# A transformer block on one core: states of batches 4 to 7 made two groups ahead, behind the output products of the next batch

## The chip, the core and the metric

The kernel runs on one NeuronCore of a Trainium2 chip. The metric is the device time of one execution in microseconds (us), the median of the runs. In names, PE is TensorE (matmul), PEld its weight loads, DVE is VectorE, ACT is ScalarE, POOL is GpSimd and SP is SyncE, whose queue issues nearly all the transfers here. [...]

## The reference

Linear attention without softmax, a norm per head, and then a gated feed-forward layer. Cut to what matters:

```python
def _attn_ref(q, k, v, g_norm):                    # (8 batches, 8 heads, 576 rows, 64)
    kv = np.einsum('bhsd,bhse->bhde', k, v)        # the state: 64 x 64 per batch and head
    out = np.einsum('bhsd,bhde->bhse', q, kv)      # the output products
    rms = np.sqrt(np.mean(out * out, axis=-1, keepdims=True) + 1e-06)
    return out / rms * g_norm

def _moe_ref(x, w_gate, w_val, w_out, rms_g):      # x: (4608, 512)
    rms = np.sqrt(np.mean(x * x, axis=-1, keepdims=True) + 1e-06)
    xn = x / rms * rms_g
    g = xn @ w_gate                                # 512 -> 1536
    silu = g * (1.0 / (1.0 + np.exp(-g)))
    val = xn @ w_val                               # 512 -> 1536
    return silu * val @ w_out                      # 1536 -> 512
```

The 4608 rows are the 8 batches of 576 rows, with the 8 heads of 64 side by side.

## The kernel before

**Groups.** The feed-forward layer works on groups of 512 rows. Group n, for n from 0 to 7, is the first 512 rows of batch n; group 8 is the 64 last rows of all eight batches together. Group 0 and the start-up have their own code; the change and the steps of the prediction lie in the end of group 0 and in groups 1 to 8, which run in the loop at L990.

**Units.** A group has 12 units of up products (`Ffn.up`, L471) and 4 of down products (`Ffn.down`, L554). Unit j makes 128 of the 1536 columns: four matmuls into a gate bank `g_ps`, four into a value bank `v_ps` (L477), each 128x128 weights on 512 columns. ACT makes `silu` from the gate bank (L482), and DVE multiplies it with the value bank into `h_sb` (L483). The gate and the value banks rotate in twos (`gps_pool`, `vps_pool`), so unit j+2 can't write its gate bank before ACT has read that of unit j, nor its value bank before DVE has read that of unit j. Each of the 4 down units is 12 matmuls into a bank `o_ps` (L529), copied by ACT to `o_sb` (L104, called from L537).

**Attention of the next group, in between.** While group n runs, the attention of batch n+1 is made in pieces, in steps that stand behind the units. `steps[u]` lists what is emitted after unit u. The order is written out by hand (a manual schedule), and each engine takes its instructions in the order in which they are emitted.

- `kv_products` (L277): the state, 72 small matmuls of 64x64 tiles (L286) from `kb` and `vb` into two banks. `kv_copy` (L291) then copies it to `kv_all`, half by ACT and half by DVE, in two copies of 64 rows each (L295).
- `o_products` (L305): 32 small matmuls with 64 rows of weights (L326), from `qt` (q turned) and `kv_all`, into two `att_ps` and two `o_ps` banks.
- `put_squares` and `put_rows` (L336, L343): ACT reads those banks twice, for squares and for the rows. `sums` (L351): DVE makes a product and a sum from the squares (L355, L356). `head`, `guess`, `root` and `scale` (L358 to L375) are the norm on DVE, and `x_rows` (L377) turns the result by transfers into `xnt`, the input of group n+1.

Before the change, in groups 2 to 6 the state of batch n+1 is made behind unit 1 and its output products behind unit 2. In group 1 it is units 2 and 4. Group 8's attention, the `tail`, has no state of its own, since it uses those of all batches.

**Inputs.** In step 2 of group n, `load_batch` loads q, k and v of batch n+2 in fp32 into three of seven stage buffers. In steps 11 to 15 of the same group ACT casts them to bf16: q in step 11, k in 12 and 13, v in 14 and 15. The bf16 k and v have two buffers each, for even and for odd batches.

Of the kernel before, what the change touches and what calls it, by code (L numbers as in the profile page):

```python
# [10 lines left out]
FP32 = mybir.dt.float32  # L11
# [9 lines left out]
def kernel(  # L21
# [14 lines left out]
    B, H, S, D = q.shape  # L36
# [8 lines left out]
    NS = d_model // 128  # L45
# [5 lines left out]
    def pool(name, bufs, **kw):  # L51
        return ctx.enter_context(tc.tile_pool(name=name, bufs=bufs, **kw))
# [16 lines left out]
    gps_pool = pool("gps", 2, space=PS)  # L69
    vps_pool = pool("vps", 2, space=PS)  # L70
    ops_pool = pool("ops", 2, space=PS)
    att_pool = pool("att", 2, space=PS)
# [3 lines left out]
    PE, DVE, SC, GP = nc.tensor, nc.vector, nc.scalar, nc.gpsimd  # L76
# [22 lines left out]
    def stage(n=2048):  # L99
        return stage_pool.tile([128, NS * C * D], FP32, name="st")[:, 0:n]  # L100

    def cast(engine, dst, src):
        if engine is SC:
            engine.copy(out=dst, in_=src)  # L104
        else:
            engine.tensor_copy(out=dst, in_=src)  # L106
# [7 lines left out]
    def alloc_kv(b, name):  # L114
        raws[b, name] = stage(NS * C * D).rearrange("p (j x) -> p j x", j=NS)

    def load_kv(b, name, queue, js=slice(0, NS)):
        view = srcs[name][b].rearrange("h s d -> (h s d)").rearrange("(j p x) -> p j x", j=NS, p=128)
        queue.dma_start(out=raws[b, name][:, js, :], in_=view[:, js, :])

    def cast_kv(b, name, j, engine):

        cast(engine, bufs[b][name][:, j].rearrange("p c d -> p (c d)"), raws[b, name][:, j, :])
# [7 lines left out]
    def load_q(b):  # L131
        st = stage()
        raws[b, "q"] = st
        for hs in (slice(0, 4), slice(4, 8)) if b == 1 else (slice(0, H),):
            nc.sync.dma_start(
                out=st.rearrange("p (h x) -> p h x", h=H)[:, hs],
                in_=q[b, hs, 0:MAIN, :].rearrange("h (p t) d -> p h (t d)", t=T),
            )

    def alloc_q(b):  # L140
        bufs[b]["q"] = qb_pool.tile([128, T, H, D], BF16, name="qb")
# [10 lines left out]
    def cast_q(b, i, engine):  # L152

        cast_heads(b, i, 2, 4, engine)

    def load_batch(b):
        load_q(b)
        for name in ("k", "v"):
            alloc_kv(b, name)
            load_kv(b, name, nc.sync)  # L160
# [34 lines left out]
    def load_wo(blk, parts=(0, 2)):  # L195
        if ("o", blk) not in w_st:
            w_st["o", blk] = stage().rearrange("p (c d) -> p c d", d=d_model)
        for i in parts:
            nc.sync.dma_start(
                out=w_st["o", blk][:, i : i + 2, :], in_=wo_view[:, 4 * blk + i : 4 * blk + i + 2, :]  # L200
            )
# [66 lines left out]
    class Att:  # L268
# [5 lines left out]
            self.sq = {}  # L274
            self.qt = None

        def kv_products(self):  # L277

            self.kv_ps = [att_pool.tile([128, 2, D], FP32, name="att_ps") for _ in range(2)]
            kb, vb = bufs[self.n]["k"], bufs[self.n]["v"]  # L280
            for a in range(2):
                for c in range(C):
                    for x in range(2):
                        for g in range(2):
                            rows, to = slice(g * D, g * D + D), slice((g ^ x) * D, (g ^ x) * D + D)
                            PE.matmul(  # L286
                                self.kv_ps[x][to, a, :], lhsT=kb[rows, 2 * a + x, c, :], rhs=vb[rows, 2 * a + x, c, :],
                                start=(a == 0 and c == 0), stop=(a == 1 and c == C - 1),
                            )
# [372 lines left out]
    def state0(j, dummies):  # L662
        ps = att_pool.tile([128, 512], FP32, name="att_ps")
        warm(ps, max(dummies, 1), 512 if dummies else 128)
        kv_pair(ps[:, 0:128], j)
        return ps
# [38 lines left out]
    kv0 = state0(0, 0)  # L705
# [96 lines left out]
    load_q(1)  # L802
    load_wo(1)
    load_wo(2)
    load_batch(2)

    def broadcast_gsq():
        ps = att_pool.tile([128, 512], FP32, name="att_ps")
# [86 lines left out]
    def f_x(c, x, engine):  # L895
        bank = att_pool.tile([128, NS, 128], BF16, name="att_ps")
        to_rows(x, 1, c, bank, engine)

    pools = ("ops", "ops", "g", "v")

    def down_part(c, lo, hi):
        ffn.down_products(c, lo, hi, pools[c])
# [44 lines left out]
    atts = {b: Att(b) for b in range(2, B + 1)}  # L947
    for c in range(T):
        atts[2].q_rows(c)
    down_part(1, 8, 12)  # L950
    f_x(0, xs[0], SC)
    f_x(1, xs[1], SC)
# [9 lines left out]
    def load_q_tails():  # L962
        st = stage().rearrange("p (c x) -> p c x", c=T)
        for b in range(B):
            u = b % 2
            nc.sync.dma_start(
                out=st[u * TAIL : (u + 1) * TAIL, b // 2].rearrange("r (h d) -> r h d", h=H),
                in_=q[b, :, MAIN:S, :].rearrange("h r d -> r h d"),
            )
        tails_q["raw"] = st  # L970
        tails_q["b"] = qb_pool.tile([128, T, H, D], BF16, name="qb").rearrange("p t h d -> p t (h d)")

    def cast_q_tails(i, engine):
        dst, src = (tails_q[nm].rearrange("p c (h d) -> p c h d", h=H) for nm in ("b", "raw"))
        cast(engine, dst[:, :, place(i) : H : 4, :], src[:, :, i:H:4, :])
# [7 lines left out]
    def turn_q_tails(c):  # L983
        if c == 0:
            tails_q["t"] = qt_pool.tile([128, NS, MAIN], BF16, name="qt").rearrange("p j (c t) -> p c j t", c=T)
        nc.sync.dma_start_transpose(out=tails_q["t"][:, c], in_=tails_q["b"][:, c, :])
# [3 lines left out]
    for n in range(1, B + 1):  # L990
        ffn = Ffn(n)
        steps = {u: [] for u in range(NF + T)}
        if n + 2 < B:
            steps[2].append(lambda n=n: load_batch(n + 2))
        if n == B - 3:
            load_q_tails()
        if n == 1:
            steps[0] += [lambda i=i: cast_kv(2, "k", i, DVE) for i in (2, 3)]
            steps[0] += [lambda i=i: cast_kv(2, "v", i, GP) for i in (0, 1)]
            steps[1] += [lambda i=i: cast_kv(2, "v", i, DVE) for i in (2, 3)]  # L1000
        if n == 3:
            steps[3] += [cross_states]
        if n < B:
            a = atts[n + 1]
            kv0, o0 = (2, 4) if n == 1 else (1, 2)
            if not a.tail:
                steps[kv0] += [a.kv_products, a.kv_copy]
            steps[o0] += [a.o_products]
            for i in range(2):
                u = o0 + 2 * i  # L1010
                steps[u] += [lambda a=a, i=i: a.put_squares(i)]
                steps[u + 1] += [lambda a=a, i=i: a.put_rows(i)]
                for c in range(2):
                    steps[u + i + c] += [lambda a=a, c=2 * i + c: a.sums(c)]
            late = 2 * int(n == 1)
            steps[8 + late] += [a.head]
            steps[9 + late] += [a.guess, a.root]
            for c in range(T):
                steps[10 if c == 0 and not late else 11] += [lambda a=a, c=c: a.scale(c), lambda a=a, c=c: a.x_rows(c)]
        b = n + 2  # L1020
        if b < B:
            steps[10] += [lambda b=b: alloc_q(b)]
            for i in range(T):
                steps[11] += [lambda b=b, i=i: cast_q(b, i, SC)]
            for i in range(NS):
                steps[12 + i // 2] += [lambda b=b, i=i: cast_kv(b, "k", i, SC)]
                steps[14 + i // 2] += [lambda b=b, i=i: cast_kv(b, "v", i, SC)]
            for c in range(T):
                steps[13].append(lambda b=b, c=c: atts[b].q_rows(c))
        if b == B:  # L1030
            for i in range(T):
                steps[11] += [lambda i=i: cast_q_tails(i, SC)]
            for c in range(T):
                steps[13].append(lambda c=c: turn_q_tails(c))
        for unit in range(NF + T):
            if unit < NF:
                ffn.up(unit)
            elif n == B and unit == NF + T - 1:
                ffn.down_last(unit - NF)
            else:  # L1040
                ffn.down(unit - NF)
            for step in steps[unit]:
                step()
# [30 lines left out]
```

## Time and profile before

| what | value |
|---|---|
| time, median of 3 runs | 319.03 us (318.98 to 319.62) |
| span of the profiled execution | 317.6 us |
| granted TensorE clock, mean | 0.998 |
| start of groups 2, 3, 4, 5, 6, 7, 8 | 87.82, 120.39, 152.97, 185.54, 218.11, 250.68, 282.53 us |
| up and down matmuls (L477, L529), ns of one in the records | 379 |
| start to start of such matmuls in a row | 216 ns |
| one silu on ACT (L482) | 597 ns |
| one product on DVE (L483) | 684 ns |
| one sum on DVE (L356) | 1220 ns |
| one copy of half a state's half, ACT / DVE | 260 / 288 ns |
| one cast of k or v on ACT, 128x576 | 673 ns |

How to read it: a matmul's record lasts 379 ns because records of matmuls overlap; what a matmul costs in a row is the 216 ns from one start to the next. A group of 144 such matmuls needs 31.1 us, and groups 2 to 6 start 32.57 us apart, so that about 1.5 us of a group is something else.

### The profile page before, as it was taken

The numbers are of one execution on the slowest core, as the hardware profiler recorded it, in microseconds if no ns is written. First come the engines' busy times: TensorE is split into PE (matmuls) and PEld (weight loads), VectorE is DVE, ScalarE is ACT, GpSimd is POOL, SyncE is SP. The second block draws the span as 40 slices with busy tenths as digits, with TensorE's granted clock in tenths as the row PEclk, the third lists the DMA queues.
The fourth block names the chain that finished last, engine by engine and source line by source line (L and its number), as shares of the span: only waits on it lengthen the run. The fifth ranks groups of instructions, "written<-read, shape, count | busy, mean of one in ns | idle before, by whom it ended". The sixth has DMA issues, their size and how long they took to land.

```text
span 317.6 us, 5996 instructions
## 1 busy us (share of the span) xinstructions
PE 308.5 (97%) x2334; PEld 150.3 (47%) x2371; DVE 181.3 (57%) x378; ACT 175.6 (55%) x323; POOL 21.5 (7%) x46
## 2 busy tenths in 40 slices
PE   7899999999999999999999999999999999999995
PEld 3575446444444444444444444444444444444443
DVE  3776768679339922893289327941795079504310
ACT  3577367485667465746683768376745374233321
POOL 1174351100000000000000000000000000000000
PEclk9999999999999999999999999999999999999999
DMA  7999999685369267904790489939002710230014
GB/s 266 358 385 388 375 375 333 145 275 215 90 180 344 86 138 187 369 9 108 189 378 22 98 172 207 354 66 181 22 0 60 140 66 3 57 141 3 0 33 100
DMA packets 60712, 54.95 MB, mean 173 GB/s; under 512 B 36232, under 2 KB 45708, under 8 KB 60684
## 3 DMA queue, kind: packets, MB, share of 16 engines
q1 hardware_dynamic: 60304, 53.92, 56.7%
q10 hardware_dynamic: 380, 0.66, 0.6%
q8 instruction: 18, 0.29, 0.4%
q14 instruction: 10, 0.08, 0.1%
HBM read 37.75 MB, written 9.44 MB: 149 GB/s over the span
## 4 chain that ended last, share of the span: by engine, by line
PE 90%; DMA 5%; SPq 1%; another core or an unknown queue 1%; issue 1%; POOL 1%; DVE 0%; ACT 0%
PE v_ps L477 28%; PE g_ps L477 28%; PE o_ps L529 26%; DMA st<-in_moe_w_val_dram 3%; DMA st<-in_q_dram 2%; PE att_ps L286 2%; PE v_ps L529 1%; PE g_ps L529 1%; DMA out_dram<-o_sb 1%; PE att_ps L326 1%; PE o_ps L494 1%; POOL wv_sb L191 1%; PE o_ps L326 0%; PE att_ps L262 0%
## 5 line engine op out<-in xcount | busy, mean ns | idle before, releaser
L483 DVE TENSOR_TENSOR h_sb<-silu,v_ps 128x512 bf16<-128x512 bf16 x104 | 71.1, 684 | 99.9 <-ACT silu L482 68.1
L477 PE MATMUL v_ps<-xnt,wv_sb 128*128 128x512 bf16 x409 | 106.2, 379 | 0.7
L477 PE MATMUL g_ps<-xnt,wg_sb 128*128 128x512 bf16 x398 | 104.6, 379 | 0.7
L482 ACT ACTIVATE silu<-g_ps 128x512 bf16<-128x512 f32 x104 | 62.1, 597 | 70.1 <-PE g_ps L477 58.4
L529 PE MATMUL o_ps<-wo_sb,h_sb 128*128 128x512 bf16 x386 | 86.8, 379 | 0.4
L477 PEld LDWEIGHTS <-wv_sb 128*128 128x128 bf16 x416 | 40.7, 98 | 49.1
L529 PEld LDWEIGHTS <-h_sb 128*128 128x128 bf16 x420 | 40.6, 98 | 47.6 <-issue 0.4
L477 PEld LDWEIGHTS <-wg_sb 128*128 128x128 bf16 x416 | 39.5, 98 | 46.4
L104 ACT COPY o_sb<-o_ps 128x512 f32<-128x512 f32 (+1 forms) x34 | 19.6, 581 | 40.2 <-PE o_ps L529 36.6
L373 DVE TENSOR_TENSOR xna<-outa,s1y 128x512 bf16<-128x512 bf16 x28 | 17.9, 685 | 0.0
L104 ACT CAST qb<-st 128x512 bf16<-128x512 f32 (+1 forms) x30 | 16.2, 603 | 3.0 <-DMA st<-in_q_dram 3.0
L104 ACT CAST vb<-st 128x576 bf16<-128x576 f32 x25 | 15.7, 673 | 3.4 <-DMA st<-in_v_dram 3.4
L356 DVE TENSOR_REDUCE ssq<-sq 128x16 f32<-128x1024 bf16 x14 | 17.1, 1220 | 0.5
L356 DVE TENSOR_REDUCE ssq<-sqt 128x16 f32<-128x1024 bf16 x14 | 17.1, 1220 | 0.5
L104 ACT CAST kb<-st 128x576 bf16<-128x576 f32 x20 | 12.5, 673 | 0.0
L341 ACT ACTIVATE sq<-att_ps 128x512 bf16<-128x512 f32 x14 | 7.6, 594 | 4.3 <-PE att_ps L326 3.6
L355 DVE TENSOR_TENSOR sq<-sq,gsq 128x512 bf16<-128x512 bf16 x14 | 5.9, 422 | 4.9 <-ACT sq L341 4.9
L629 PE MATMUL att_ps<-kv_all 128*128 128x512 bf16 (+1 forms) x21 | 7.5, 486 | 1.2 <-DVE sel L618 1.2
L106 DVE CAST kb<-st 128x576 bf16<-128x576 f32 x12 | 6.1, 527 | 3.6 <-DMA st<-in_k_dram 3.5
L106 POOL CAST wo_sb<-st 128x512 bf16<-128x512 f32 x12 | 7.3, 635 | 7.4 <-DMA st<-in_moe_w_out_dram 7.4
L341 ACT ACTIVATE sqt<-o_ps 128x512 bf16<-128x512 f32 x14 | 7.6, 597 | 0.0
L347 ACT CAST outa<-o_ps 128x512 bf16<-128x512 f32 x14 | 7.5, 591 | 0.0
(150 smaller groups left out, 181.5 us busy)
## 6 DMA issues: line engine op xcount, KB each, us to landing
st<-in_k_dram SPq DMA_DIRECT2D x7, 1152.0 KB, 10.5
st<-in_v_dram SPq DMA_DIRECT2D x7, 1152.0 KB, 12.6
out_dram<-o_sb SPq DMA_DIRECT2D x14, 512.0 KB, 3.1
st<-in_q_dram SPq DMA_DIRECT2D x6, 1024.0 KB, 7.2
st<-in_moe_w_out_dram SPq DMA_DIRECT2D x6, 512.0 KB, 10.4
st<-in_moe_w_gate_dram SPq DMA_DIRECT2D x4, 512.0 KB, 10.4
st<-in_moe_w_val_dram SPq DMA_DIRECT2D x4, 512.0 KB, 9.8
st<-in_k_dram SPq DMA_DIRECT2D x4, 288.0 KB, 4.0
```

The source lines that it names most:

```text
L104: engine.copy(out=dst, in_=src)
L106: engine.tensor_copy(out=dst, in_=src)
L286: PE.matmul(self.kv_ps[x][to, a, :], lhsT=kb[rows, 2 * a + x, c, :], rhs=vb[rows, 2 * a + x, c, :], start=(a == 0 and c == 0), stop=(a == ...
L341: SC.activation(out=self.in_place(self.sq[i][:, 0], g), in_=bank, func=ACT.Square)
L347: SC.copy(out=self.in_place(rows, g), in_=bank)
L356: DVE.reduce_sum(out=self.ssq[:, c], in_=sq, axis=AX.X)
L373: DVE.tensor_tensor(out=self.xna[c], in0=self.outa[c], in1=self.alpha[:, c, :].to_broadcast([128, H, D]), op=OP.mult)
L477: PE.matmul(ps, lhsT=wt[:, s, j * 128 : (j + 1) * 128], rhs=x[:, s, :], start=(s == 0), stop=(s == NS - 1),)
L482: SC.activation(out=silu, in_=g_ps, func=ACT.Silu)
L483: DVE.tensor_tensor(out=self.h[:, j, :], in0=silu, in1=v_ps, op=OP.mult)
L529: PE.matmul(self.o_ps[c], lhsT=self.h[:, j, c * 128 : (c + 1) * 128], rhs=wo_sb[:, j, :], start=(j == 0), stop=(j == NF - 1),)
L629: PE.matmul(ps[:, 0:w], lhsT=warm_sb[:, 0:128], rhs=warm_sb[:, 0:w], start=True, stop=True, skip_group_check=True)
```

## The change

In groups 2 to 5 the state is now made one group earlier than before and in another place: group n makes the state of batch n+2 (batches 4 to 7) directly behind the output products of batch n+1, in one stretch of small matmuls in place of two. The two banks for it are not `att_ps` any more, which the output products hold at that point, but one gate bank and one value bank. `kv_copy` follows at once, and so stands ahead of `put_squares` on ACT and of `sums` on DVE. Groups 6 and 7 make no state.

For this, k and v have to come one batch earlier. `load_batch` is split: step 2 of group n loads q of batch n+2 and k and v of batch n+3, which are also cast in group n, in steps 12 to 15. The pair of batch 3 is loaded at the end of group 0, cast by ACT in steps 8 to 10 of group 1, and its state is made in step 12 of group 1, behind the first down unit, in `att_ps` banks.

The purpose is to join two stretches of small matmuls into one, and to have the state ready long before the output products need it.

```diff
-    def load_batch(b):
-        load_q(b)
+    def load_pair(b):
         for name in ("k", "v"):
             alloc_kv(b, name)
             load_kv(b, name, nc.sync)
...
-        def kv_products(self):
+        def kv_products(self, pools=((att_pool, "att_ps"),) * 2):
 
-            self.kv_ps = [att_pool.tile([128, 2, D], FP32, name="att_ps") for _ in range(2)]
+            self.kv_ps = [p.tile([128, 2, D], FP32, name=nm) for p, nm in pools]
...
-    load_batch(2)
+    load_q(2)
+    load_pair(2)
...
     for c in range(T):
         atts[2].q_rows(c)
+    load_pair(3)
     down_part(1, 8, 12)
...
         if n + 2 < B:
-            steps[2].append(lambda n=n: load_batch(n + 2))
+            steps[2].append(lambda n=n: load_q(n + 2))
+        if n + 3 < B:
+            steps[2].append(lambda n=n: load_pair(n + 3))
...
         if n == 1:
...
+            steps[2] += [atts[2].kv_products, atts[2].kv_copy]
+            for i in range(NS):
+                steps[8 + i // 2] += [lambda i=i: cast_kv(3, "k", i, SC)]
+                steps[9 + i // 2] += [lambda i=i: cast_kv(3, "v", i, SC)]
+            steps[12] += [atts[3].kv_products, atts[3].kv_copy]
...
         if n < B:
             a = atts[n + 1]
-            kv0, o0 = (2, 4) if n == 1 else (1, 2)
-            if not a.tail:
-                steps[kv0] += [a.kv_products, a.kv_copy]
+            o0 = 4 if n == 1 else 2
             steps[o0] += [a.o_products]
+            if 1 < n < B - 2:
+                s = atts[n + 2]
+                steps[o0] += [lambda s=s: s.kv_products(((gps_pool, "g_ps"), (vps_pool, "v_ps"))), s.kv_copy]
...
-            for i in range(NS):
-                steps[12 + i // 2] += [lambda b=b, i=i: cast_kv(b, "k", i, SC)]
-                steps[14 + i // 2] += [lambda b=b, i=i: cast_kv(b, "v", i, SC)]
             for c in range(T):
                 steps[13].append(lambda b=b, c=c: atts[b].q_rows(c))
+        if b + 1 < B:
+            for i in range(NS):
+                steps[12 + i // 2] += [lambda b=b, i=i: cast_kv(b + 1, "k", i, SC)]
+                steps[14 + i // 2] += [lambda b=b, i=i: cast_kv(b + 1, "v", i, SC)]
```

In the changed kernel the lines up to the loop stand one earlier: L285 for the state's matmuls, L325 for the output products, L476 for the up products.

## The prediction

> **What bounds the kernel now.** I read the page's first part, then the waits of TensorE alone, then the timeline of one steady group, because the page says who is busy, the waits say whether the busy engine ever waits for another, and only the timeline shows how close it comes to waiting.
>
> From the page, busy time by engine:
>
> ```profile
> PE 308.5 (97%) x2334; PEld 150.3 (47%) x2371; DVE 181.3 (57%) x378; ACT 175.6 (55%) x323; POOL 21.5 (7%) x46
> ```
>
> TensorE is at 97%, no other engine at 60%. The waits of TensorE (engine, line, for whom: us in total, times, longest), first and last line of six:
>
> ```profile
> PE att_ps L629 <- DVE sel L618: 1.2, 1, 1.2
> ...
> PE v_ps L503 <- POOL wv_sb L191: 0.2, 1, 0.2
> ```
>
> All six are lines of the start-up of batch 0, 3.1 us in all. In groups 1 to 8 TensorE waits for nobody. So two things can change the time there: what TensorE itself does, and a new wait. Group 3 in the timeline (start, us, engine, line, instruction), around its units 1 to 6:
>
> ```profile
> 122.98 1.03 PE L477 MATMUL v_ps<-xnt,wv_sb 128*128 128x512 bf16 x4
> ...
> 123.94 0.78 PE L286 MATMUL att_ps<-vb,kb 64*64 64x64 bf16 x72
> ...
> 124.65 1.04 PE L477 MATMUL g_ps<-xnt,wg_sb 128*128 128x512 bf16 x3
> 124.77 0.53 ACT L104 CAST kv_all<-att_ps 64x128 bf16<-64x128 f32 x2 [0.98 <-PE att_ps L286]
> ...
> 126.48 0.41 PE L326 MATMUL att_ps<-kv_all,qt 64*128 64x64 bf16 x16
> ...
> 126.72 0.40 PE L326 MATMUL o_ps<-kv_all,qt 64*128 64x64 bf16 x16
> 126.92 1.09 ACT L341 ACTIVATE sq<-att_ps 128x512 bf16<-128x512 f32 x2 [0.60 <-PE att_ps L326]
> ...
> 127.06 1.04 PE L477 MATMUL g_ps<-xnt,wg_sb 128*128 128x512 bf16 x4
> ...
> 128.04 0.42 DVE L355 TENSOR_TENSOR sq<-sq,gsq 128x512 bf16<-128x512 bf16 x1 [0.69 <-ACT sq L341]
> ...
> 131.82 1.39 DVE L483 TENSOR_TENSOR h_sb<-silu,v_ps 128x512 bf16<-128x512 bf16 x2
> ...
> 133.11 1.03 PE L477 MATMUL v_ps<-xnt,wv_sb 128*128 128x512 bf16 x4
> ```
>
> The reader is to see two islands of small matmuls (L286 the state, L326 the output products) with one unit between them, and behind them one chain: ACT squares (126.92), DVE sums from 128.04, then the two products of L483 at 131.82, units 4 and 5. Unit 6's value matmuls (133.11) write the bank that unit 4's product has read; that product ends at 131.82 + 0.68 = 132.50. The slack is 0.61 us, the smallest of any unit in every group from 2 to 6 (next smallest: unit 7's product before unit 9's values, 0.72). On DVE everything from 128.04 to that product runs without a gap.
>
> **What the Trainium skill says.** "TensorEngine Tiling (Array Packing)", Key Properties: changing the tiling mode, not just the tile, drains TensorE. The trace agrees: the last matmul in front of the state starts at 123.63 and streams for 0.216, yet the state starts at 123.94, 0.095 late; the same 0.095 stands before the output products, and each island's last small matmul is followed only after 0.12, where matmuls of L326 follow in pairs every 0.03. "PSUM — Partial Sum Buffer", Engine vs sequencer instructions: ScalarE's and VectorE's queues are strict FIFO. The trace agrees as far as it can: in no group does a ready silu overtake a waiting copy. No other page bears on it.
>
> **The change, part by part.** U3 is the start of unit 3's first matmul, the first after the output products.
>
> 1. Work of TensorE. Seven states (batches 1 to 7) of 72 matmuls before and after; only their places change. Group 1 gains one (batch 3, in step 12, between two down products), groups 2 to 5 keep one each, now right behind the output products, group 6 loses one. One island costs 0.095 to enter, 0.71 (123.94 to 124.65), and 0.01 in the first full matmul: 0.81. Group 1's gain and group 6's loss cancel.
>
> 2. Merged islands, groups 2 to 5. Before: 0.095 + 0.71 + 0.01 + 0.095 + 0.573 (126.48 to 127.06) + 0.01 = 1.49; with 144 matmuls of 0.216 this makes 32.59, and groups start every 32.57 us. After: 0.095 + 0.45 (output products up to their last start) + x + 0.71 + 0.01. The switch x from a 64*128 to a 64*64 mode is nowhere in the trace: between 0.03 (no drain) and 0.12 (as the exits). The page on tiling names any change of mode, so I take 0.12. **Gain 0.105 a group, 0.42 us in four** (at most 0.81).
>
> 3. ACT. kv_copy now stands in front of the squares in its queue, and waits for a state that ends only just before U3. Behind it are queued the squares, unit 3's silu and the row copies; DVE's sums wait for the squares. The copies ran from 0.12 after the first full matmul (124.77 against 124.65) for 0.53, so now U3+0.12 to U3+0.65. Before, the squares began at U3-0.13. The copies work on 64 rows and the second began 0.01 after the first ended, while full-height ACT instructions overlap by 0.10; what follows a 64-row copy at once the trace doesn't show, so the squares begin between U3+0.55 and U3+0.72; I take U3+0.66, as the copies do. **Squares and sums come 0.79 us later against TensorE** (0.68 to 0.85). DVE's own copies of the state (0.59) end by U3+0.75, before the squares, and cost nothing.
>
> 4. The new wait. Everything on DVE from the first sum to unit 4's product moves by that 0.79, and 0.61 was free. DVE to TensorE takes 0.05 (a DVE copy ends at 22.38, the matmuls of L494 start at 22.43). Unit 6's values therefore wait 0.79 + 0.05 - 0.61 = **0.23 us a group, 0.94 in four** (0.12 to 0.29 each). Unit 7's product had 0.11 more slack and TensorE is then 0.23 later, so there is no second wait; unit 3's had 1.07. ACT has caught up by unit 5's silu (0.15 idle in front of it before), and unit 4's silu ends near U3+3.7, where DVE comes to its product only at U3+5.6. The silu bank's slack is 1.79.
>
> 5. Banks. The state takes unit 1's gate and value banks; they were read by 124.8 here, over 1.5 us before it. Unit 4's gate bank, at U3+1.74, needs the copies done at U3+0.65. Nothing.
>
> 6. Group 1. Eight more casts on ACT in units 8 to 10, at 0.573 start to start. Unit 8's silu is at 71.62 and waits for TensorE. Queue after it: two casts, silu 9 at 73.35, four casts, silu 10 at 76.13 (before 75.07), two casts, silu 11 at 77.77 (76.80). Unit 11's product follows at 78.5 to 79.2 instead of 77.76 to 78.44; the down products need it at 77.46 + 11 x 0.216 = 79.84. Hidden, 0.6 to spare. The norm of batch 2 is 0.76 later, so its transposes end near 87.7 instead of 86.9, and group 2 now starts at 88.63. The transposes of q for the next group end near 93.8, needed at 94.25. Hidden, but with 0.45 to spare only.
>
> 7. Loads. k and v of batch 3 (2.36 MB) go out at 59.8, ahead of the outputs of batch 0. At the 401 GB/s that loads reach from 70 to 74 they take 5.9 us, so the loads behind them end near 82 instead of 76.7; the transposes move data from 82.7 on. Just hidden. Later groups load the same amount, group 5 less.
>
> Sum: -0.42 + 0.94 = +0.52, so 319.03 + 0.52 = **319.55 us**.
>
> **The rivals.**
> - **The queues absorb it** (25%): ACT overlaps the copies with the squares, or the switch x is free. The slack of 0.61 speaks against, the overlap of 0.10 between full-height instructions for it. With a wait of 0.05 and x of 0.03: -0.81 + 0.2 = 318.4; without any wait and with a drained switch 318.6; at best 318.2.
> - **The wait in unit 6** (55%): as above. With 0.12 to 0.29 for the wait and 0.12 for x it is +0.06 to +0.74, 319.1 to 319.8.
> - **Group 1 and its transposes too** (20%): one of the margins of parts 6 and 7 (0.45 and under 1 us) is not there, and TensorE stands for 0.3 to 1 us at the start of group 2 or before its output products. For it speaks that the DMA line is full until 76; against it, that each margin was positive. +0.52 + 0.6 = 320.15.
>
> **How the numbers follow.** The likeliest gives 319.55. The first rival lies around 318.4; a fifth of its cases and a tenth on the far side of the third are left out: 318.3 to 320.2. Faster by 0.2% means under 318.39: 0.15 of the first rival's 0.25. Slower means over 319.67: the third's 0.20 and about a quarter of the second's, 0.15. The rest, 0.50, is within 0.2%.
>
> **What would show it.** Part 2: the small matmuls of L285 follow those of L325 after about 0.12, and 0.105 us a group are gone. Parts 3 and 4: squares starting about 0.66 after unit 3's first matmul, and a line of TensorE's waits, v_ps on DVE h_sb, four times near 0.23. If that line is missing, the first rival holds; if it stands in other units or is over 0.4, DVE is slower than I think. Part 6: a wait of TensorE on a DMA near 88 to 95 makes the third rival. The forecast is wrong if group 1 or 6 changes by more than the 0.81 of a moved state, or if a group from 2 to 5 changes by more than 0.3.

## The result: slower by 0.9%, and where it shows in the profile after

| | before | after |
|---|---|---|
| time, median (lowest to highest), 6 runs each | 319.40 us (318.98 to 319.96) | 322.37 us (321.64 to 322.79) |
| ratio to before, 95% interval | | 1.0090 (1.0072 to 1.0107) |
| span of the profiled execution | 317.6 us | 320.7 us |

The forecast was 319.55 us, in a range up to 320.2. The medians lie 2.97 us apart.

I read the starts of the groups first, since a group without waits has one fixed length. The length is the difference of two starts in the trace, in us:

| group | 1 | 2 | 3 | 4 | 5 | 6 | 7 |
|---|---|---|---|---|---|---|---|
| before | 32.57 | 32.57 | 32.57 | 32.57 | 32.57 | 32.57 | 31.85 |
| after | 33.38 | 34.31 | 32.95 | 32.83 | 32.98 | 31.76 | 31.85 |
| difference | +0.81 | +1.74 | +0.38 | +0.26 | +0.41 | -0.81 | 0 |

The sum is +2.79, nearly all of the loss. The +0.81 of group 1, which gains a state, and the -0.81 of group 6, which loses one, cancel, as forecast. Group 2 is the large one, and groups 3 to 5 each lose a third of a microsecond.

On the page, the line of busy times hardly differs from that of before. It can't tell what happened:

```profile
PE 308.8 (96%) x2338; PEld 150.7 (47%) x2371; DVE 180.2 (56%) x378; ACT 174.3 (54%) x323; POOL 21.5 (7%) x46
```

The waits of TensorE can (engine, line, for whom: us in total, times, longest). Two lines are new against before:

```profile
PE o_ps L325 <- DMA qt<-qb: 1.3, 1, 1.3
...
PE v_ps L476 <- DVE h_sb L482: 1.0, 4, 0.3
```

The second is the forecast wait of unit 6's values, four times. The first is one wait at the start of group 2's attention: output products that stand for q's transpose. The other lines are of the start-up.

**The wait in unit 6**, in the timeline of group 4 (start, us, engine, line, instruction):

```profile
162.02 0.22 PE L285 MATMUL g_ps<-vb,kb 64*64 64x64 bf16 x2
...
162.72 1.04 PE L476 MATMUL g_ps<-xnt,wg_sb 128*128 128x512 bf16 x3
162.84 0.53 ACT L104 CAST kv_all<-g_ps 64x128 bf16<-64x128 f32 x2 [1.56 <-PE v_ps L285]
...
163.40 1.09 ACT L340 ACTIVATE sq<-att_ps 128x512 bf16<-128x512 f32 x2
...
164.51 0.42 DVE L354 TENSOR_TENSOR sq<-sq,gsq 128x512 bf16<-128x512 bf16 x1 [1.04 <-ACT sq L340]
...
164.97 1.22 DVE L355 TENSOR_REDUCE ssq<-sq 128x16 f32<-128x1024 bf16 x1
...
166.22 0.69 DVE L482 TENSOR_TENSOR h_sb<-silu,v_ps 128x512 bf16<-128x512 bf16 x1
...
167.28 1.22 DVE L355 TENSOR_REDUCE ssq<-sq 128x16 f32<-128x1024 bf16 x1
...
168.42 1.27 DVE L482 TENSOR_TENSOR h_sb<-silu,v_ps 128x512 bf16<-128x512 bf16 x2
...
169.15 1.02 PE L476 MATMUL v_ps<-xnt,wv_sb 128*128 128x512 bf16 x4 [0.21 <-DVE h_sb L482]
```

U3 is at 162.72. ACT stands idle (the 1.56 in brackets) until the state is there, copies it, and comes to the squares at U3+0.67, where they began at U3-0.13 before. Everything on DVE behind them moves along, and unit 4's product, the first of the two at 168.42, ends just before TensorE goes on at 169.15. The 0.21 in brackets is short of the delay, because records of matmuls overlap. Taken from starts, the wait is 0.37 us.

**The wait in group 2**, in the chain that ended last (start, us, what):

```profile
90.57 1.26 SPq L299
91.83 0.04 issue
91.87 4.10 DMA qt<-qb
95.97 0.05 issue
96.02 0.29 PE o_ps L325 x8
```

SyncE issues the four transposes of q one after another, 1.3 us apart. The last one is issued at 91.87 and takes 4.10 us to land, where 2.5 is the median in this trace. TensorE had begun the output products at 94.18, did the 24 that need the first three transposes, and stood still for the last eight until 96.02. The kernel before (first two lines) and the changed one (last two) in the timeline:

```profile
93.91 0.41 PE L326 MATMUL att_ps<-kv_all,qt 64*128 64x64 bf16 x16
94.15 0.40 PE L326 MATMUL o_ps<-kv_all,qt 64*128 64x64 bf16 x16
...
94.43 0.28 PE L325 MATMUL o_ps<-kv_all,qt 64*128 64x64 bf16 x8
96.02 0.29 PE L325 MATMUL o_ps<-kv_all,qt 64*128 64x64 bf16 x8 [1.31 <-DMA qt<-qb]
```

Without a wait, the 32 small matmuls take 0.45 us from first to last start; here they take 1.93, so the wait is 1.48 us.

What held this transpose is in the records of the single transfers. The view of DMA queues counts them by kind (packets, MB, share of 16 engines):

```profile
## 3 DMA queue, kind: packets, MB, share of 16 engines
...
q8 instruction: 18, 0.29, 0.4%
```

These are 18 packets of 16 KB each. One of them ran from 93.10 to 94.47, in the middle of this transpose. In the kernel before, the nearest 16 KB packet began at 95.57, over 2 us after q's last transpose had landed (93.42).

### The profile page after: what moved, and what is told of

Same layout as the page of the kernel before. It is cut to its first block, busy times and chain, and to the rows that moved or that the text cites. A ratio compares the mean times of both kernels' runs of the same rounds, so it can differ in the third digit from the quotient of the medians.

```text
span 320.7 us, 5995 instructions
## 1 busy us (share of the span) xinstructions
PE 308.8 (96%) x2338; PEld 150.7 (47%) x2371; DVE 180.2 (56%) x378; ACT 174.3 (54%) x323; POOL 21.5 (7%) x46
## 4 chain that ended last, share of the span: by engine, by line
PE 87%; DMA 6%; SPq 1%; issue 1%; DVE 1%; another core or an unknown queue 1%; POOL 1%; ACT 0%; DVEq 0%; POOLq 0%
PE v_ps L476 28%; PE o_ps L528 26%; PE g_ps L476 26%; DMA st<-in_moe_w_gate_dram 2%; DMA st<-in_q_dram 2%; DMA qt<-qb 1%; DVE h_sb L482 1%; PE g_ps L493 1%; SPq L299 1%; PE v_ps L528 1%; PE g_ps L528 1%; PE att_ps L285 1%; PE g_ps L285 1%; DMA out_dram<-o_sb 1%
## 5 line engine op out<-in xcount | busy, mean ns | idle before, releaser
L476 PE MATMUL v_ps<-xnt,wv_sb 128*128 128x512 bf16 x413 | 106.3, 379 | 1.4 <-DVE h_sb L482 1.0
L476 PE MATMUL g_ps<-xnt,wg_sb 128*128 128x512 bf16 x398 | 104.6, 379 | 0.7
L476 PEld LDWEIGHTS <-wv_sb 128*128 128x128 bf16 x416 | 40.6, 98 | 50.9 <-issue 2.3
L476 PEld LDWEIGHTS <-wg_sb 128*128 128x128 bf16 x416 | 39.9, 98 | 47.4
```

The source lines that it names most:

```text
L476: PE.matmul(ps, lhsT=wt[:, s, j * 128 : (j + 1) * 128], rhs=x[:, s, :], start=(s == 0), stop=(s == NS - 1),)
```

## The experiments

Each ratio is to runs of the kernel before on the same chip.

Theory A: the copies of the state, ahead of the squares on ACT, make the wait in unit 6. Its rival B: the banks (the PSUM buffers that take the results of matmuls), or the early loads. For the wait in group 2, I began with theory C (the casts of batch 3 on ACT make everything behind them late) against D (the loads are in the way).

**State first.** In the loop, for groups 2 to 5:

```diff
-            steps[o0] += [a.o_products]
             if 1 < n < B - 2:
                 s = atts[n + 2]
                 steps[o0] += [lambda s=s: s.kv_products(((gps_pool, "g_ps"), (vps_pool, "v_ps"))), s.kv_copy]
+            steps[o0] += [a.o_products]
```

> The changed kernel, with the state of batch n+2 made and copied in front of the output products in the same slot of groups 2 to 5, instead of behind them: one stretch of small matmuls still, in the same gate and value banks, with the same loads and casts. Theory A (the copies that stand ahead of the squares and wait for the last small matmul cost 0.37 to 0.46 us in each of four groups): the copies now run while the output products are made, squares start near U3+0.1 instead of U3+0.67 to U3+0.79, the waits of v_ps on h_sb go, and the time falls by 1.6 to 1.7 us, from 322.4 to about 320.7. Rival B (the gate and value banks in the state's hands, or the early loads, cost the time): within 0.3 us of 322.4, since banks and loads are as in the changed kernel. Either way the wait of the output products on q's transpose in group 2 (1.3 us) stays.

Measured: 320.10 us, ratio 1.0024 (1.0011 to 1.0037). No wait of v_ps on h_sb is left. Banks and loads are the same as in the changed kernel, so B falls. It is 0.6 us better than expected, because the wait in group 2 shrank as well, to 0.91 us: behind the state, the products come 0.7 us later and meet q's transpose later. Groups 3 and 4 take 32.47 us, group 5 takes 32.59: the matmuls of its state need 0.71 us from first to last start in place of 0.58.

**Copies behind the squares.** The sharper test, since TensorE's order stays as it was:

```diff
-                steps[o0] += [lambda s=s: s.kv_products(((gps_pool, "g_ps"), (vps_pool, "v_ps"))), s.kv_copy]
+                steps[o0] += [lambda s=s: s.kv_products(((gps_pool, "g_ps"), (vps_pool, "v_ps")))]
...
                 steps[u] += [lambda a=a, i=i: a.put_squares(i)]
+                if i == 0 and 1 < n < B - 2:
+                    steps[u] += [atts[n + 2].kv_copy]
```

> The changed kernel with nothing but the place of kv_copy altered in groups 2 to 5: it is emitted behind the first pair of squares, so TensorE's order is that of the changed kernel to the instruction. Theory A (order on ACT is the cause): squares start in front of U3 again, unit 4's product ends in time, the waits of v_ps on h_sb go: 320.7 us (320.5 to 320.9). If it was DVE that was late for a reason of its own (its copies of the state, placed ahead of the sums in both): the waits stay at 0.3 or more each and the time within 0.3 us of 322.4.

Measured: 320.56 us, ratio 1.0036 (1.0020 to 1.0053). The timeline of its group 4:

```profile
162.09 1.08 ACT L340 ACTIVATE sq<-att_ps 128x512 bf16<-128x512 f32 x2 [0.60 <-PE att_ps L325]
...
162.93 1.04 PE L476 MATMUL g_ps<-xnt,wg_sb 128*128 128x512 bf16 x4
...
163.06 0.53 ACT L104 CAST kv_all<-g_ps 64x128 bf16<-64x128 f32 x2
163.09 0.59 DVE L106 CAST kv_all<-v_ps 64x128 bf16<-64x128 f32 x2 [0.57 <-PE v_ps L285]
...
163.71 0.43 DVE L354 TENSOR_TENSOR sq<-sq,gsq 128x512 bf16<-128x512 bf16 x1
```

U3 is at 162.93 here. The squares now start 0.84 us ahead of it, and the copies run when the squares are done. The first sum is at U3+0.78 instead of U3+1.79. Groups 3 to 5 take 32.47, 32.47 and 32.48 us: no wait, and 0.105 less than before. Theory A is shown: with the copies ahead of the squares on ACT, each of four groups loses 0.37 to 0.51 us. The wait in group 2 stays, 1.43 us.

**Casts of batch 3 on GpSimd.** In group 1:

```diff
-                steps[8 + i // 2] += [lambda i=i: cast_kv(3, "k", i, SC)]
-                steps[9 + i // 2] += [lambda i=i: cast_kv(3, "v", i, SC)]
+                steps[8 + i // 2] += [lambda i=i: cast_kv(3, "k", i, GP)]
+                steps[9 + i // 2] += [lambda i=i: cast_kv(3, "v", i, GP)]
```

> The changed kernel with the eight casts of batch 3 in group 1 on GpSimd (0.67 us each in the trace) instead of ACT; all else stays, the loads too. Theory C (the casts on ACT hold up silu 9 to 11 and so the norm of batch 2 and all transposes behind it by 0.75 us, and that lets group 2's output products run into q's last transpose): the wait of o_ps on qt in group 2 goes, 322.4 falls by 1.3 to 1.5 us to 321.0, and the four waits in unit 6 stay. Rival D (the loads of batch 3's k and v fill the queues and the transposes are late for that): the wait stays, within 0.3 us of 322.4.

Measured: 321.64 us, ratio 1.0071 (1.0054 to 1.0089). A miss: the wait is still 1.45 us in the profile. The last transpose of q was issued 0.39 us earlier than in the changed kernel, counted from the group's start, but it landed even more slowly. Its chain:

```profile
92.00 4.46 DMA qt<-qb
96.46 0.05 issue
96.51 0.29 PE o_ps L325 x8
```

The trace has sixteen landings for each transpose. Fifteen came from 94.43 to 94.62; the sixteenth came at 96.46. A 16 KB packet of queue q8 ran from 94.44 to 95.36. The Trainium skill has both halves of this. "DMA: Bandwidth & Descriptors", Why a DMA increments its semaphore by 16 and not by 1: each engine that takes part adds its own one, and only the full 16 means that the data is there. "Runtime: NRT & Kernel Launch", Instruction fetch mechanics: instructions are fetched in blocks of 16 KiB, 256 instructions, over a DMA queue. The trace agrees: the packets have 16,384 bytes, and TensorE is on average at 247 more of its recorded instructions from one to the next, in the kernel before (278 in front of the first of the 18 packets, 4481 in front of the last; singly, 157 to 342). The page calls the cost of crossing a block mostly hidden. Here it isn't, if the packet is what delays the transpose, which the runs below test. That the packet held the engine of the sixteenth landing is inferred: the trace doesn't say which engine a packet ran on.

So C was too simple, and C' takes its place: the packet delays the transpose, and comes roughly with TensorE's place in its program. Making the transposes a little earlier doesn't get them out of its way.

**Both edits together** (casts on GpSimd, copies behind the squares):

> Both edits together: casts of batch 3 on GpSimd and the state's copies behind the first squares. Theories A and C, if they account for all of it: TensorE waits for nobody after the start-up, 322.4 - 1.4 - 1.7 = 319.3 us; from the other side, the kernel before less the 0.42 us of the joined stretches: 319.0. If there is a third cause, 319.8 or more.

Measured: 319.85 us, ratio 1.0011 (1.0002 to 1.0020). By what was expected, 319.8 or more means a third cause. What the run has over the 319.0 is about what is left of the wait in group 2, 0.76 us: the landing still took 4.01. Groups 3 to 5 take 32.47 us each.

**The packet moved.** In the start-up, where TensorE warms up:

```diff
-    warm(warm_ps, 9)
+    warm(warm_ps, 8)
+    warm(warm_ps, 15, 32)
```

> The changed kernel with its nine start-up warming matmuls of 512 columns written as eight of 512 and fifteen of 32: 14 more matmuls with 14 weight loads on TensorE, at a time when it has nothing else to do. Nothing else changes. In the traces one 16 KB packet of an instruction queue comes per about 250 instructions of TensorE, so 28 more at the start should bring each such packet 28 instructions earlier, 3.0 us in a row of up products: the one that stands at 93.1 (end 94.5) in the changed kernel, and holds one of the DMA engines while q's last transpose of batch 3 lands, comes near 90. Theory C' (that packet is what makes the transpose land 4.1 us after its issue instead of 2.5): the wait of o_ps on qt falls from 1.4 to 0 to 0.2, the time from 322.4 to 321.0. Rival D (the 0.75 us lag of the transposes, or traffic, does it alone): the wait stays over 1 us, the time within 0.3 us of 322.4. The four waits in unit 6 stay in both.

Measured: 321.50 us, ratio 1.0052 (1.0033 to 1.0071). The packet came 1.28 us after the start of group 2 instead of 4.19, moved by 2.9 where 3.0 were computed. The chain:

```profile
89.49 2.04 SPq L299
91.53 0.04 issue
91.58 2.54 DMA qt<-qb
94.12 0.05 issue
94.17 0.29 PE o_ps L325 x8
```

The landing is at 2.54 us again, so C' holds: the packet made it 4.1. The wait fell only by half, to 0.70, and not to 0 to 0.2. The packet now lies over an earlier transpose, and SyncE's issue of the one after that takes 2.04 us instead of 1.25 (first line), so that the last one goes out 0.78 us later. That the held engine is what stopped the issue is inferred from the times.

**The packet moved, in the kernel with both edits:**

> The same 28 instructions at the start of the kernel that has batch 3's casts on GpSimd and the state's copies behind the squares (319.85, still a wait of 0.6 to 0.7 on q's transpose). Theory C': that wait goes, 319.1, which is 0.4 below the kernel before, the gain of the joined stretches. Rival D: within 0.2 us of 319.85.

Measured: 318.89 us, ratio 0.9976 (0.9967 to 0.9986). The landing takes 2.56 us, the wait 0.25. From the start of group 1 on, its trace is 0.23 us shorter than that of the kernel before, and the interval says 0.45 to 1.05. Part of the rest lies outside the profiled span: the device time is longer than the span by 1.78 to 1.80 us at the median in the four kernels with casts on GpSimd, and by 2.01 to 2.05 in all others. So about 0.2 us of the gain over before belongs to these casts and not to the joined stretches; no run tells why.

**Group 2's products later.** One line, so that they stand behind unit 3 in group 2:

```diff
-            o0 = 4 if n == 1 else 2
+            o0 = 4 if n == 1 else 3 if n == 2 else 2
```

> The changed kernel, with the output products and the state of group 2 alone one unit later (behind unit 3), 1.73 us after where they were. Both theories of the hand-over from group 1 to 2 say that the wait of the output products on q's transpose (1.3 us) goes, since it lands in time whatever held it up: 321.0 us, with the four waits on h_sb kept (group 2's now in front of unit 7's values). If the wait only moves to another place (the norm of group 2 starts later, its transposes then end too late for group 3), 322 or more.

Measured: 320.78 us, ratio 1.0033 (1.0023 to 1.0044). The transpose landed late here too (4.51 us), but of the wait 0.16 us are left, and groups 3 to 5 still have theirs (32.83, 32.83, 32.96).

**All three edits**: casts on GpSimd, copies behind the squares, group 2's products later.

> Casts of batch 3 on GpSimd, the state's copies behind the squares, and group 2's output products and state one unit later: no wait of TensorE is left behind the start-up, 319.85 less 0.7 makes 319.1 us, 0.4 under the kernel before. If group 2's norm is too late for group 3, 319.6 or more.

Measured: 318.87 us, ratio 0.9973 (0.9963 to 0.9984), level with the 318.89 of both edits with the packet moved. TensorE's waits, first and last line; those between are of the start-up as well:

```profile
PE att_ps L628 <- DVE sel L617: 1.2, 1, 1.2
...
PE g_ps L397 <- ACT qt L104: 0.2, 1, 0.2
```

Groups 2 to 5 take 32.47 us each. By the trace, groups 1 to 8 are 0.47 us shorter than before, just outside the interval (0.51 to 1.18 us below); with the 0.2 us outside the span it is inside.

**Old place, new loads.** The state of batch n+2 behind unit 1, in `att_ps` banks:

```diff
-                steps[o0] += [lambda s=s: s.kv_products(((gps_pool, "g_ps"), (vps_pool, "v_ps"))), s.kv_copy]
+                steps[1] += [s.kv_products, s.kv_copy]
```

> The changed kernel, with the state of batch n+2 made behind unit 1 of groups 2 to 5, in att_ps banks, where the kernel before makes that of batch n+1: two stretches of small matmuls again, but with the early loads, the casts of batch 3 on ACT in group 1 and its state in step 12. Theory A and C': groups 3 to 5 take 32.57 us as in the kernel before, and no v_ps waits for h_sb; group 2 has its output products 0.81 later than in the changed kernel (6.1 us after its start), so of the wait on q's transpose 0 to 0.8 us are left, by where the 16 KB packet falls: 0 to 0.8 above the kernel before, 319.5 to 320.4. If early loads or casts cost something beside that, groups 3 to 5 are longer than 32.6.

Measured: 319.62 us, ratio 1.0003 (0.9991 to 1.0015). Groups 3 to 5 take 32.57 us as before, group 2 32.73. So the early loads and the eight casts on ACT cost nothing but these 0.16 us, and the loss of the change comes with the new place of the state. The landing took 3.59 here, with a packet on it. It is the two runs with the packet moved that speak against D: the same loads, and a landing of 2.5.

**The start-up edit alone**, in the kernel before:

> The kernel before with the start-up edit alone (eight warming matmuls of 512 and fifteen of 32 in place of nine of 512). It measures what that edit is worth by itself in the two kernels that carry it, where group 1 began 0.8 to 1.1 us earlier than in the others. If that was chance, within 0.2 us of the kernel before; if the edit shortens the start-up, 0.3 to 0.8 below it. Groups 1 to 8 stay at 32.57, 31.85 and 31.85 us each.

Measured: 319.81 us, ratio 1.0006 (0.9992 to 1.0021). The edit is worth nothing by itself; that group 1 began early in single profiles is the scatter of start-ups (54.5 to 56.6 us over all traces). All groups stay as they were.

**The hand-over in one table**, from the traces, in us. Times of issue and packet are counted from the start of group 2. The wait is what the output products take over 0.45.

| kernel | last q transpose issued | 16 KB packet | landing took | products begin | wait |
|---|---|---|---|---|---|
| before | 3.08 | 7.74 to 8.67 | 2.52 | 6.09 | 0 |
| after | 2.96 | 4.19 to 5.56 | 4.10 | 5.28 | 1.48 |
| state first | 2.97 | 5.04 to 6.02 | 4.23 | 5.98 | 0.91 |
| copies behind | 2.95 | 4.17 to 5.47 | 4.06 | 5.28 | 1.43 |
| GpSimd casts | 2.57 | 5.01 to 5.93 | 4.46 | 5.28 | 1.45 |
| both | 2.33 | 4.31 to 5.24 | 4.01 | 5.28 | 0.76 |
| packet moved | 3.74 | 1.28 to 2.62 | 2.54 | 5.28 | 0.70 |
| both, packet moved | 3.27 | 0.77 to 2.15 | 2.56 | 5.28 | 0.25 |
| products later | 2.96 | 5.37 to 6.29 | 4.51 | 7.00 | 0.16 |
| all three edits | 2.31 | 4.70 to 6.05 | 2.54 | 7.00 | 0 |
| old place | 2.97 | 2.73 to 4.14 | 3.59 | 6.09 | 0.16 |

The landing is 2.5 us wherever the packet is out of the way, whatever the loads, and 3.6 to 4.5 where it begins from 0.2 us before the issue to 2.4 us after it. At 2.4 us it can go either way: the products-later row and the row of all three edits differ by 0.02 us in that, and one landing is late and the other isn't.

The packet's place isn't exact. In seven of these kernels (after, state first, copies behind, GpSimd casts, both, products later, all three edits) TensorE has the same instructions up to about 5.28, and yet the packet begins anywhere from 4.17 to 5.37. The 28 instructions moved it by 2.9 us from the changed kernel, by 3.5 from the kernel with both edits and by 2.1 from the kernel before, where 3.0 were computed. So whether packet and transpose meet is in part chance. There is one trace of each kernel; how far the packet scatters from run to run isn't shown.

## Why the prediction was wrong, point by point

**Right.** The work of TensorE (part 1: group 1 +0.81, group 6 -0.81). The joined stretches (part 2): 0.105 us a group, measured as 32.572 less 32.467. The switch x: the state follows the products after 0.12. The delay of squares (part 3): U3+0.67 in group 4, 0.66 forecast. Banks and loads (parts 5 and 7): nothing, shown by the runs with the state first and in the old place.

**Part 4, the mechanism right, the size not (0.8 us of the error).** The forecast wait was 0.23 us a group. It is 0.37, 0.48, 0.37 and 0.51 in groups 2 to 5 (length less 32.467, in group 2 also less 1.48), 1.73 in place of 0.94. Two terms of the sum were short:

- "Everything on DVE from the first sum to unit 4's product moves by that 0.79": it moves by 0.93. Before, unit 3's product begins 0.08 before the sum ahead of it ends; after, 0.03 behind its end (166.19 to 166.22 in the lines above). It isn't the silu, which came 0.8 us before in the kernel with the copies behind, where the same 0.03 stands. It goes with the copies of the state. From group 1 on, in the twelve traces, the product behind a sum begins 0.03 after its end in all 36 cases where such a copy is the last thing that DVE has read from a bank, and 0.08 to 0.09 before its end in all 300 others; unit 4's product above is one of these (168.42, and the sum ends at 168.50). In the kernel before, unit 2's product stood between the copies and the sums. Why a copy of 64 rows takes the overlap away stays open.
- In groups 3 and 5 ACT and DVE begin the copies of the state 0.12 to 0.14 us later after its last matmul than in groups 2 and 4, at the same order and timing of TensorE. It isn't the parity of the group: with the packet moved, group 5 doesn't show it, and with the products later group 3 doesn't. This stays open too. An untested lead: in the nine kernels that make the state next to the output products, there are 13 groups where the copies, or the state itself, are late by 0.1 us or more. In 12 of them a 16 KB packet begins 0.6 to 1.8 us after the state's last matmul; but it does so in three groups that aren't late as well.

**Part 6, the step that failed (1.5 us of the error).** "The transposes of q for the next group end near 93.8, needed at 94.25. Hidden, but with 0.45 to spare only." Two things are wrong in it.

First, the 0.45 doesn't come out of the forecast's own figures. In the kernel before, the last transpose landed at 93.42; with the lag of 0.76 from the casts that is 94.18, and 0.07 are left. The trace of the changed kernel agrees: issued at 91.87, with a landing of 2.54 the transpose would have been there at 94.41 + 0.05, and the eight products need it at about 94.5. Still hidden, by next to nothing. In the kernel before the margin was 0.8 us (landed 93.42, needed near 94.25). The lag used it up, since the need stayed near where it was: group 1 is longer by 0.81, and the products, with no state in front of them, stand earlier in group 2 by 0.81.

Second, the forecast put at nothing what else runs on the DMA engines but loads and outputs, and so took a landing of 2.5 us as given. It took 4.10. The 16 KB packet, in the kernel before well behind the landing, fell right on it. Group 1 has 144 more instructions of TensorE (72 matmuls and their weight loads), and group 2 has 144 fewer in front of its products, so the ends of the blocks lie elsewhere against the transposes. The runs that move the packet show that it is the cause of the long landing; that the 144 instructions moved it is argued from the count.

**The sum.** Forecast: -0.42 + 0.94. Measured: -0.42 + 1.73 + 1.48 = +2.79. The third rival named the place ("TensorE stands for 0.3 to 1 us ... before its output products"), and its sign, a wait on a DMA between 88 and 95 us, came true (from 94.7 on), but at a fifth of the chance and with 0.6 us for 1.48, and it was built on the forecast for unit 6, which was itself 0.8 us short. The two errors are independent, as the runs that mend one and leave the other show, and both go the same way: each started from a slack that was nearly used up, and counted only the delays that it knew.

## What to carry to other kernels

In an in-order queue, try what waits for the newest result of TensorE behind what doesn't: here, moving the copies behind the squares, with the matmuls untouched, took back 1.8 us. When work moves between groups, look at the slack of each transfer whose reader comes earlier; here 0.1 us was left, and of a delay of 1.6 us nearly all was paid (1.48). A cheap cure is distance: one unit more between transpose and reader, in the one group that needs it, left 0.16 of that wait.

## What the runs showed of the hardware that I had not expected

- A block of instructions, 16 KB in 0.9 to 1.4 us, delays the landing of a transpose under way from 2.5 to between 3.6 and 4.5 us, in seven kernels. With the casts on GpSimd, the last 256-byte packet of the transpose had ended at 94.17, before the block began at 94.44; still one landing came 1.10 us after the block's end, when 15 of 16 had come by 94.62. In two of the seven kernels one landing is late like this, in the other five all sixteen are late together. How one block delays all of them stays open. Earlier in the chain the issue is held up instead (2.04 us in place of 1.25).
- Where these blocks fall depends on how many instructions TensorE has had: 28 more at the start moved one by 2.1 to 3.5 us, in three pairs of kernels.
- A product on DVE begins 0.08 to 0.09 us before the end of the sum ahead of it (300 of 300), but 0.03 after it where the copy of a state, 64 rows, is DVE's last reading of a bank (36 of 36). It cost 0.11 us a group.
